# The second layer of the last two token chunks as seven block products, five of them in float32r

## The chip, the cores and the metric

The kernel runs on one core of a Trainium2 chip, as one launch. A core has TensorE (PE in the profile; its weight loads are listed apart, as PEld), VectorE (DVE), ScalarE (ACT), GpSimd (POOL) and SyncE (SP), each with its own queue of instructions, two on-chip memories (SBUF, and PSUM, which matmuls write) and DMA queues to the device's memory. The metric is the device time of one execution in microseconds.

## The reference

Attention over 8 batches of 8 heads, 576 positions of 64 values each, with a local mask for heads 0 to 3 and a strided one for heads 4 to 7, followed by a feed-forward layer on the 4608 tokens of 512 values:

```
scores = scale * np.matmul(q, k.transpose(0, 1, 3, 2))
...
attn = np.exp(scores)
attn = attn / (np.sum(attn, axis=-1, keepdims=True) + 1e-09)
...
h = x @ w_in            # 4608 x 512  times  512 x 2048
r = np.maximum(h, 0.0)
g = r * r
return (g @ w_out)      # 4608 x 2048  times  2048 x 512
```

The change concerns only the last line, `g @ w_out`, for the last 1024 tokens. Inputs and output are float32.

## The kernel before

The attention leaves its result `x`, transposed and in bf16, in four tiles `xt` (128 of the 512 values by 4608 tokens). The feed-forward layer takes the tokens in nine chunks of 512. For each chunk, `mm1` (lines 731 to 746) makes one group for each of 16 slices of 128 hidden values: four matmuls of 512 columns into one of two PSUM banks, `nc.scalar.activation(r, ph, AF.Relu)` on ACT into one of four `r` buffers, and, queued one group later by `later(1, ...)`, the square on DVE into `g[:, ff, :]`. `g` has two buffers, so that chunk c + 2 writes where chunk c was. Then `mm2` (lines 750 to 769) makes the second layer: for each of four blocks of 128 tokens, 16 matmuls of 512 columns, four in a group, with a slice of `g` as the stationary operand and `w_out_b[:, ff, :]` as the moving one; ACT copies the bank to a `y` buffer and SP's queue sends it to the output.

`last_y` (lines 775 to 790) does the last 128 tokens of the last chunk in pieces of 256, 128 and 128 columns, so that the first pieces leave while the last is computed.

The whole program is one list of groups (lines 947 to 972). With c from 2 on, groups 32c to 32c + 15 are chunk c's first layer, and the next 16 are its second layer. The attention of later batches is placed between the groups by a table written out by hand, `PLAN` (lines 23 to 165): at each group number, the steps to be issued ahead of it. Every engine runs its instructions in the order in which this list issues them. The last steps of the plan are at groups 188 (`G7`, the last local scores), 197 to 202 (`s7.0` to `s7.2`, the last strided scores), 198 to 206 (`D28` to `E29`) and 209 to 217 (`x7.0` to `x7.2`, the last strided values). From group 218 on there is only the feed-forward layer: the second layer of chunk 6 ends at group 223, chunk 7 is groups 224 to 255, and chunk 8 groups 256 to 287.

All tiles of the attention (staging, transposed q and k, `es`, `vl_all`, `vbds`, `kbds` and others) live in pools that stay open to the end of the kernel. PSUM has eight banks: `banks["ph"]` holds two, used by `mm1` and by most of `mm2`; `banks["pt"]` holds the others, used by the attention's steps and free at the end.

Lines that the prediction names: `L739` is the matmul of the first layer, `L761` and `L786` those of the second, `L745` the relu, `L746` the square, `L765` and `L789` the copies of results out of PSUM, `L583`, `L607` and `L621` matmuls of the steps `G`, `s` and `x`, `L705` a step of the local attention on DVE, `L426` the last load on POOL's queue, and `L884`, `L886` and `L898` the mask and the clearing of tiles on POOL early in the kernel.

Of the kernel before, what the change touches and what calls it, by code (L numbers as in the profile page):

```python
# [8 lines left out]
FP32 = mybir.dt.float32  # L9
BF16 = mybir.dt.bfloat16  # L10
AF = mybir.ActivationFunctionType
ALU = mybir.AluOpType
# [155 lines left out]
def kernel(  # L168
# [9 lines left out]
    nc = tc.nc  # L178
    B, H, S, D = q.shape
    d_model, d_ff = moe_w_in.shape  # L180
    T = B * S
# [4 lines left out]
    NL = S // QL  # L186
# [4 lines left out]
    VP = 72  # L191
    SR = 80
    NP2 = STRIDE // 2
    NG = 5
    NB = NP2 + NG + 1
    W3 = 3 * NA
    RW = STRIDE * D
    ER = S + 32

    singles = ctx.enter_context(tc.tile_pool(name="singles", bufs=1))  # L200
    qk_in = ctx.enter_context(tc.tile_pool(name="qk_in", bufs=4))
    qkT = ctx.enter_context(tc.tile_pool(name="qkT", bufs=4))
    v_st = ctx.enter_context(tc.tile_pool(name="v_st", bufs=1))
    rv_pool = ctx.enter_context(tc.tile_pool(name="rv_pool", bufs=3))
    small = ctx.enter_context(tc.tile_pool(name="small", bufs=4))
    xl_pool = ctx.enter_context(tc.tile_pool(name="xl_pool", bufs=4))
    g_pool = ctx.enter_context(tc.tile_pool(name="g_pool", bufs=2))
    r_pool = ctx.enter_context(tc.tile_pool(name="r_pool", bufs=4))
    y_pool = ctx.enter_context(tc.tile_pool(name="y_pool", bufs=4))

    PS = bass.MemoryType.PSUM
    strTs = {nm: ctx.enter_context(tc.tile_pool(name=f"strT{nm}", bufs=n)) for nm, n in (("q", 2), ("k", 1))}
# [25 lines left out]
    NV = 4  # L238
# [4 lines left out]
    vl_all = singles.tile([128, NV, 2, NL, VP], BF16, name="vl")  # L243
    vls = [vl_all[:, i] for i in range(NV)]

    vbds = [singles.tile([128, NB, 128], BF16, name=f"vb{i}") for i in range(2)]
    kbds = [singles.tile([128, NB, 128], BF16, name=f"kb{i}") for i in range(2)]
    ones_bd = singles.tile([128, 128], BF16)
    mask_bd = singles.tile([128, 1, W3], BF16)
    str_rows_t = {nm: singles.tile([SR, RW], BF16, name=f"{nm}_t") for nm in "qk"}  # L250
    kTl = [singles.tile([128, 32 + S], BF16, name=f"kTl{i}") for i in range(NV)]
    es01 = singles.tile([128, 4 * ER], BF16, name="e01")
    es = [es01[:, 0:2 * ER], es01[:, 2 * ER:]] + [singles.tile([128, 2 * ER], BF16, name=f"e{i}") for i in (2, 3)]
# [213 lines left out]
    def later(n, fn, key=None):  # L467
        pending.append((clock[0] + n, key, fn))

    def run_due(test):  # L470
        due = [x for x in pending if test(x)]
        for x in due:
            pending.remove(x)
        for x in sorted(due, key=lambda x: x[0]):
            x[2]()

    def tick():
        clock[0] += 1
        run_due(lambda x: x[0] <= clock[0])
# [229 lines left out]
    def step_E(u, copy=None):  # L709
# [14 lines left out]
        copy(xt[p][:, b * S:(b + 1) * S], px)  # L724
        st.pop(u)

    gs = {}

    phs = {}

    def mm1(c, ff, kks=range(4), order=range(4), pool=None):
        if ff == 0 and c not in gs:
            gs[c] = g_pool.tile([128, 16, 512], BF16, name="g_sb")
        g = gs[c]
        if kks[0] == order[0]:
            phs[ff] = bank(pool or "ph")
        ph = phs[ff]
        for kk in kks:
            nc.tensor.matmul(ph, w_in_b[:, kk, 128 * ff:128 * (ff + 1)],  # L739
                             xt[kk][:, 512 * c:512 * (c + 1)],  # L740
                             start=(kk == order[0]), stop=(kk == order[-1]))
        if kks[-1] != order[-1]:
            return
        r = r_pool.tile([128, 512], BF16, name="r")
        nc.scalar.activation(r, ph, AF.Relu)  # L745
        later(1, lambda: nc.vector.tensor_tensor(g[:, ff, :], r, r, op=ALU.mult))  # L746

    ys = {}

    def mm2(c, i, pool=None):  # L750
        j, part = divmod(i, 4)
        g = gs[c]
        if part == 0:
            if pool == "pt":
                ys[c, j] = bank("pt")
                banks["pt"].remove(ys[c, j])
            else:
                ys[c, j] = bank(pool or "py")
        py = ys[c, j]
        for ff in range(4 * part, 4 * part + 4):  # L760
            nc.tensor.matmul(py, g[:, ff, 128 * j:128 * (j + 1)], w_out_b[:, ff, :],  # L761
                             start=(ff == 0), stop=(ff == 15))
# [8 lines left out]
    NCH = T // 512  # L771
    A, V, G = nc.scalar.copy, nc.vector.tensor_copy, nc.gpsimd.tensor_copy
    ENG = {"a": A, "v": V, "g": G}

    def last_y(c, j, i):
        g, r0 = gs[c], 512 * c + 128 * j
        if i == 0:
            ys[c, j] = y_pool.tile([128, 512], FP32, name="y")
        y = ys[c, j]
        cols = (slice(0, 256), slice(0, 256), slice(256, 384), slice(384, 512))[i]  # L780
        ffs = (range(0, 8), range(8, 16), range(16), range(16))[i]
        if i != 1:
            ys[c, j, i] = bank("ph")
        py = ys[c, j, 0 if i == 1 else i]
        for ff in ffs:
            nc.tensor.matmul(py[:, cols], g[:, ff, 128 * j:128 * (j + 1)], w_out_b[:, ff, cols],  # L786
                             start=(ff == 0), stop=(ff == 15))
        if i:
            (V if i == 3 else A)(y[:, cols], py[:, cols])  # L789
            (nc.scalar if i == 2 else nc.sync).dma_start(out=out[r0:r0 + 128, cols], in_=y[:, cols])  # L790

    def warm(n):
        if n:
# [153 lines left out]
    groups = []  # L947

    def add(c, kind, i, pool=None):
        if kind == 0:  # L950
            groups.append(lambda: None)
        elif kind == 1:
            groups.append(lambda: mm1(c, i, pool=pool))
        elif c == NCH - 1 and i >= 12:
            groups.append(lambda: last_y(c, i // 4, i % 4))
        else:
            groups.append(lambda: mm2(c, i, pool))

    for ff in range(16):
        add(0, 1, ff, {NP: "pt", 8: "py"}.get(ff)) if ff >= NP else add(0, 0, ff)  # L960
    for part in range(4):
        for j, pool in ((0, "ph"), (1, "ph"), (2, None), (3, "pt")):
            add(0, 2, 4 * j + part, pool)
    for i in range(16):
        add(1, 1, i)
    for i in range(16):
        add(1, 2, i, "ph")
    for c in range(2, NCH):
        for i in range(16):
            add(c, 1, i)  # L970
        for i in range(16):
            add(c, 2, i, "ph")

    plan = {}
    for line in PLAN.strip().splitlines():
        n, words = line.split(":")
        plan.setdefault(int(n), []).extend(words.split())
    for n, g in enumerate(groups):
        if n == 32:
            banks["pt"] += banks.pop("py")  # L980
        for word in plan.get(n, ()):
            run_step(word)
        g()
        tick()
    for _ in range(4):
# [31 lines left out]
```

## Time and profile before

| | us |
|---|---|
| median of 3 runs | 299.06 (298.43 to 301.52) |
| the profiled execution | 299.14 |
| its span in the profile | 297.4 |
| TensorE busy | 287.8 |
| VectorE busy | 180.3 |
| ScalarE busy | 170.5 |
| GpSimd busy | 73.3 |

The span is the time from the first instruction in the trace to the last; the execution took 1.7 us more than that. A row of the page's fifth part names the line, the engine, the operation, what it writes and reads (partitions by elements, type), how often it runs, its busy time and the mean duration of one. A matmul's drawn duration is longer than its share of the stream, since matmuls are pipelined; the pace is read from start to start. In the 40 slices a digit is the busy share of a slice in tenths. A row of the timeline has a start, a length and an instruction, or several alike in one.

### The profile page before, as it was taken

Reading aid. Unit: us, or ns where it says so; the run is one execution under the profiler, and the core shown is the slowest. Engines: PE = TensorE matmul, PEld = TensorE weight load, DVE = VectorE, ACT = ScalarE, POOL = GpSimd, SP = SyncE. Lnnn points to the kernel's source line nnn. Section 1 sums busy time; section 2 is a strip of 40 time slices with the busy share of each in tenths; the row PEclk is TensorE's granted clock in tenths of the full one; section 3 lists DMA queues with packets and bytes.
Section 4 is the critical chain, followed back from the end, with each engine's and each line's share of the span. In section 5 each row is a group of like instructions: output and inputs, shape, how many; then the busy total and the mean of one; then the engine's idle time right before and its main releaser. Section 6 shows DMA issues by size and latency. Waiting matters only on the chain.

```text
span 297.4 us, 5621 instructions
## 1 busy us (share of the span) xinstructions
PE 287.8 (97%) x2112; PEld 144.6 (49%) x2148; DVE 180.3 (61%) x465; ACT 170.5 (57%) x318; POOL 73.3 (25%) x107
## 2 busy tenths in 40 slices
PE   7989999999999999999999999999999999999994
PEld 2644555544545454444454445544544444444444
DVE  5557689697777769779367936776575334004300
ACT  3758846774668636764577447744764266127411
POOL 8874743014513036065105700000000000000000
PEclk9999999999999999999999999999999999999999
DMA  7999999999999999999998999411011100020012
GB/s 146 183 207 204 189 199 189 156 224 204 168 179 179 123 164 199 160 144 188 179 128 125 177 149 145 82 55 73 35 31 47 71 37 0 35 89 20 0 71 73
DMA packets 91724, 37.38 MB, mean 126 GB/s; under 512 B 77549, under 2 KB 85831, under 8 KB 91697
## 3 DMA queue, kind: packets, MB, share of 16 engines
q0 software_dynamic: 50608, 18.33, 55.8%
q1 hardware_dynamic: 40944, 18.62, 32.3%
q8 instruction: 17, 0.28, 0.4%
q14 instruction: 11, 0.08, 0.1%
q10 hardware_dynamic: 144, 0.07, 0.1%
HBM read 37.22 MB, written 9.44 MB: 157 GB/s over the span
## 4 chain that ended last, share of the span: by engine, by line
PE 94%; DMA 2%; issue 1%; DVE 1%; ACT 0%; POOL 0%; DVEq 0%; POOLq 0%
PE psb L739 42%; PE psb L761 40%; DMA w_out_b<-in_k_dram 2%; PE psb L699 2%; PE psb L621 1%; PE psb L607 1%; PE psb L786 1%; PE psb L618 1%; PE psb L583 1%; PE psb L538 1%; PE psb L486 1%; DVE xt L668 0%; PE psb L508 0%; PE psb L333 0%; DVE x_l L688 0%
## 5 line engine op out<-in xcount | busy, mean ns | idle before, releaser
L739 PE MATMUL psb<-xt,w_in_b 128*128 128x512 bf16 x558 | 132.1, 379 | 1.2 <-DVE xt L668 0.2
L761 PE MATMUL psb<-w_out_b,g_sb 128*128 128x512 bf16 x542 | 125.3, 379 | 1.2 <-issue 0.5
L745 ACT ACTIVATE r<-psb 128x512 bf16<-128x512 f32 x144 | 85.3, 599 | 37.9 <-PE psb L739 32.8
L746 DVE TENSOR_TENSOR g_sb<-r 128x512 bf16<-128x512 bf16 x144 | 60.4, 423 | 68.5 <-ACT r L745 67.2
L739 PEld LDWEIGHTS <-w_in_b 128*128 128x128 bf16 x576 | 53.2, 97 | 58.9 <-issue 1.4
L761 PEld LDWEIGHTS <-g_sb 128*128 128x128 bf16 x560 | 52.0, 98 | 57.9 <-DVE g_sb L746 0.3
L765 ACT COPY y<-psb 128x512 f32<-128x512 f32 x35 | 20.6, 588 | 51.6 <-PE psb L761 48.6
L631 DVE TENSOR_TENSOR xt<-psb,rv 64x144 bf16<-64x144 f32 x84 | 34.0, 405 | 12.7 <-ACT rv L624 11.6
L623 ACT ACTIVATE rv<-psb 128x432 f32<-128x432 f32 (+1 forms) x21 | 10.5, 501 | 12.8 <-PE psb L618 12.8
L705 DVE TENSOR_TENSOR x_l<-psb,rinv 96x384 bf16<-96x384 f32 x28 | 15.5, 553 | 1.0
L361 POOL DMA_DIRECT2D q_t<-in_q_dram x6 | 3.3, 544 | 45.8 <-DMA qT_s<-q_t 44.9
L594 ACT ACTIVATE e<-psb 128x384 bf16<-128x384 f32 x30 | 12.0, 513 | 4.2 <-PE psb L583 4.2
L608 ACT ACTIVATE e<-psb 128x432 bf16<-128x432 f32 (+1 forms) x21 | 10.4, 496 | 4.0 <-PE psb L607 4.0
L637 DVE TENSOR_TENSOR xt<-psb,rv 64x270 bf16<-64x270 f32 (+1 forms) x28 | 11.0, 433 | 2.5 <-ACT rv L624 2.3
L290 POOL DMA_DIRECT2D q_l<-in_q_dram x16 | 12.0, 754 | 1.6 <-DMA q_l<-in_q_dram 1.4
L290 POOL DMA_DIRECT2D k_l<-in_k_dram x16 | 11.7, 736 | 1.6 <-DMA v_st<-in_v_dram 1.5
L624 ACT ACTIVATE rv<-rv 128x432 f32<-128x432 f32 (+1 forms) x21 | 11.2, 533 | 0.7
L590 DVE TENSOR_TENSOR e<-e,mask_all 128x576 bf16<-128x576 bf16 x20 | 8.4, 456 | 4.9 <-ACT e L594 4.9
L699 PEld LDWEIGHTS <-e 128*128 128x128 bf16 x168 | 8.0, 97 | 4.6
L361 POOL DMA_DIRECT2D k_t<-in_k_dram x6 | 3.2, 536 | 25.0 <-DMA kT_s<-k_t 22.9
L699 PE MATMUL psb<-vl,e 128*128 128x65 bf16 x168 | 9.0, 193 | 0.0
L607 PEld LDWEIGHTS <-kb 128*128 128x128 bf16 x154 | 6.8, 96 | 4.5
(119 smaller groups left out, 213.5 us busy)
## 6 DMA issues: line engine op xcount, KB each, us to landing
out_dram<-y SPq DMA_DIRECT2D x35, 256.0 KB, 4.2
w_out_b<-in_moe_w_out_dram POOLq DMA_DIRECT2D x4, 512.0 KB, 15.1
q_t<-in_q_dram POOLq DMA_DIRECT2D x7, 288.0 KB, 7.3
k_t<-in_k_dram POOLq DMA_DIRECT2D x7, 288.0 KB, 6.9
vl<-in_v_dram POOLq DMA_DIRECT2D x6, 288.0 KB, 7.7
v_st<-in_v_dram POOLq DMA_DIRECT2D x7, 216.0 KB, 6.8
w_in_b<-in_moe_w_in_dram POOLq DMA_DIRECT2D x2, 704.0 KB, 14.3
k_l<-in_k_dram POOLq DMA_DIRECT2D x16, 72.0 KB, 7.0
```

Of the source, the lines that this page charges most:

```text
L290: nc.gpsimd.dma_start(out=t[:, :, hh, :], in_=src[b, 2 * p + hh].rearrange("(t p) d -> p t d", p=QL))
L594: nc.scalar.activation(e[:, row, 4 * QL * i:4 * QL * (i + 1)], bk[row][i][:, 0:4 * QL], AF.Exp, scale=scale)
L624: nc.scalar.activation(rv, rv, AF.Exp, scale=-1.0)
L631: nc.vector.tensor_tensor(to[:, :, NJ * part:NJ * (part + 1), par], of, by, op=ALU.mult)
L637: nc.vector.tensor_tensor(t, of[:, g:, :, lo:lo + k], by[:, g:, :, lo:lo + k], op=ALU.mult)
L699: nc.tensor.matmul(po[:, n, :], e[:, c:c + 128], rhs[:, NL * part + n, 0:D + 1], start=True, stop=True)
L705: nc.vector.tensor_tensor(x, po[0:QL, :, 0:D], rinv[0:QL].to_broadcast([QL, NL, D]), op=ALU.mult)
L739: nc.tensor.matmul(ph, w_in_b[:, kk, 128 * ff:128 * (ff + 1)], xt[kk][:, 512 * c:512 * (c + 1)], start=(kk == order[0]), stop=(kk == order ...
L745: nc.scalar.activation(r, ph, AF.Relu)
L746: later(1, lambda: nc.vector.tensor_tensor(g[:, ff, :], r, r, op=ALU.mult))
L761: nc.tensor.matmul(py, g[:, ff, 128 * j:128 * (j + 1)], w_out_b[:, ff, :], start=(ff == 0), stop=(ff == 15))
L765: nc.scalar.copy(y, py)
```

## The change

For chunks 7 and 8 (`SEVEN`) the second layer is computed as a 2 by 2 by 2 block product with seven block multiplications. Tokens are split in pairs of 128 (t = 0, 1, within each half u of the chunk), hidden values in 0 to 1023 and 1024 to 2047, output columns in two times 256. With A11 and A12 the two hidden halves of the first 128 tokens, A21 and A22 those of the second 128, and B11 to B22 the blocks of `w_out`:

```
S1 = A21 + A22   S2 = S1 - A11   S3 = A11 - A21   S4 = A12 - S2
T1 = B12 - B11   T2 = B22 - T1   T3 = B22 - B12   T4 = B21 - T2
P1 = A11 B11  P2 = A12 B21  P6 = S2 T2  P7 = S3 T3  P4 = A22 T4  P5 = S1 T1  P3 = S4 B22
C11 = P1 + P2   C12 = P1 + P6 + P5 + P3   C21 = P1 + P6 + P7 + P4   C22 = P1 + P6 + P7 + P5
```

B21 is the lower left block, `w_out_b[:, 8:16, 0:256]`. The numbers are those of the code: products 1 and 2 have bf16 operands, `g` and `w_out_b`; the other five take operands that are sums, or a block copied to float32, held as float32r.

Five things are new:

- `weight_sums` (groups 204 to 223, one step at each) makes T1, a copy of B22, T3, T2 and T4 on POOL, in four pieces of 512 elements a partition each: 20 instructions. Before the first of them the pools of q and k (`rows`) are closed, and the new tiles take their memory; each waits for what used that memory.
- `squares` takes the place of the square in `mm1` for these chunks. For the slices 8 to 15 it makes, out of `r`, the square of the second tokens as float32r (`S["a"]`) and that of the first tokens as bf16, both on DVE, then S3 on DVE and S1, S2 and S4 on POOL, 256 elements each. Its tiles take the memory of the other attention pools (`att`).
- The first layer's order in these chunks is 0, 8, 1, 9, ..., 7, 15.
- `mm2_7` does one product of one half, eight matmuls of 256 columns, in the order 1, 2, 6, 7, 4, 5, 3, each for u = 0 and then u = 1. Products 2, 7 and 3 go on adding in the bank of the product before them on that bank. ACT copies the bank after 1 and 2; after the others DVE adds the bank and an earlier part of `y`.
- `last_y` is gone; in the last product, two additions of 128 columns and three DMAs (of 256, 128 and 128 columns) end the kernel.

```diff
     def mm1(c, ff, kks=range(4), order=range(4), pool=None):
...
         nc.scalar.activation(r, ph, AF.Relu)
+        if c in SEVEN:
+            later(1, lambda: squares(c, ff, r))
+            return
         later(1, lambda: nc.vector.tensor_tensor(g[:, ff, :], r, r, op=ALU.mult))
+
+    SEVEN = (NCH - 2, NCH - 1)
+    ts, ss = {}, {}
+
+    def weight_sums(step):
+        F32R = mybir.dt.float32r
+        if not ts:
+            rows.close()
+            late = ctx.enter_context(tc.tile_pool(name="late", bufs=1, side="right", reuse_waits="tile"))
+            for nm in ("1", "2", "3", "4", "b"):
+                ts[nm] = late.tile([128, 8, 256], F32R, name=f"t{nm}")
+        nm, i = "1b324"[step // 4], 2 * (step % 4)
...
+        if nm == "b":
+            nc.gpsimd.tensor_copy(t["b"], b22)
+            return
+        x, y = {"1": (b12, b11), "3": (b22, b12), "2": (b22, t["1"]), "4": (b21, t["2"])}[nm]
+        nc.gpsimd.tensor_tensor(t[nm], x, y, op=ALU.subtract)
+
+    def squares(c, ff, r):
+        g, i = gs[c], ff % 8
...
+        if ff < 8:
+            nc.vector.tensor_tensor(g[:, ff, :], r, r, op=ALU.mult)
+            return
+        S = {k: x[:, i] for k, x in ss.items()}
+        r = r.rearrange("p (u t c) -> p u t c", u=2, t=2)
+        a1, a2 = (g[:, k, :].rearrange("p (u t c) -> p u t c", u=2, t=2) for k in (i, ff))
+        nc.vector.tensor_tensor(S["a"], r[:, :, 1], r[:, :, 1], op=ALU.mult)
+        nc.vector.tensor_tensor(a2[:, :, 0], r[:, :, 0], r[:, :, 0], op=ALU.mult)
+        nc.vector.tensor_tensor(S["3"], a1[:, :, 0], a1[:, :, 1], op=ALU.subtract)
+        nc.gpsimd.tensor_tensor(S["1"], a1[:, :, 1], S["a"], op=ALU.add)
+        nc.gpsimd.tensor_tensor(S["2"], S["1"], a1[:, :, 0], op=ALU.subtract)
+        nc.gpsimd.tensor_tensor(S["4"], a2[:, :, 0], S["2"], op=ALU.subtract)
+
+    ORDER7 = "1 2 6 7 4 5 3".split()
+
+    def mm2_7(c, i):
+        n, u = ORDER7[i // 2], i % 2
...
+        for k in range(8):
+            a = g[:, k, t0] if n == "1" else g[:, 8 + k, t0] if n == "2" else \
+                ss[{"6": "2", "7": "3", "4": "a", "5": "1", "3": "4"}[n]][:, k, u]
+            b = w_out_b[:, k, lo] if n == "1" else w_out_b[:, 8 + k, lo] if n == "2" else \
+                ts[{"6": "2", "7": "3", "4": "4", "5": "1", "3": "b"}[n]][:, k]
+            nc.tensor.matmul(pa, a, b, start=k == 0 and n not in "273", stop=k == 7, skip_group_check=True)
+        if n in "12":
+            nc.scalar.copy((y2 if n == "1" else y1)[:, lo], pa)
+            return
...
+        if n == "3" and c == NCH - 1 and u:
+            nc.sync.dma_start(out=out[r0:r0 + 128, lo], in_=y1[:, lo])
+            for h, eng in ((0, nc.scalar), (128, nc.sync)):
+                nc.vector.tensor_tensor(to[:, h:h + 128], pa[:, h:h + 128], by[:, h:h + 128], op=ALU.add)
+                eng.dma_start(out=out[r0:r0 + 128, 256 + h:384 + h], in_=to[:, h:h + 128])
+            return
+        nc.vector.tensor_tensor(to, pa, by, op=ALU.add)
...
-        elif c == NCH - 1 and i >= 12:
-            groups.append(lambda: last_y(c, i // 4, i % 4))
+        elif c in SEVEN:
+            groups.append(lambda: mm2_7(c, i) if i < 14 else None)
...
-            add(c, 1, i)
+            add(c, 1, i // 2 + 8 * (i % 2) if c in SEVEN else i)
...
+        if 204 <= n < 224:
+            weight_sums(n - 204)
```

More of the change, by code (lines that the diff above doesn't have):

```diff
@@ L200 @@
     singles = ctx.enter_context(tc.tile_pool(name="singles", bufs=1))
[L201 to L204, printed above, removed]
     small = ctx.enter_context(tc.tile_pool(name="small", bufs=4))
-    xl_pool = ctx.enter_context(tc.tile_pool(name="xl_pool", bufs=4))
     g_pool = ctx.enter_context(tc.tile_pool(name="g_pool", bufs=2))
@@ L209 @@
     y_pool = ctx.enter_context(tc.tile_pool(name="y_pool", bufs=4))
+    att = ctx.enter_context(ExitStack())
+    rows = ctx.enter_context(ExitStack())
+    att_singles = att.enter_context(tc.tile_pool(name="att_singles", bufs=1))
+    rv_pool = att.enter_context(tc.tile_pool(name="rv_pool", bufs=3))
+    xl_pool = att.enter_context(tc.tile_pool(name="xl_pool", bufs=4))
+    row_singles = rows.enter_context(tc.tile_pool(name="row_singles", bufs=1, side="right"))
+    qk_in = rows.enter_context(tc.tile_pool(name="qk_in", bufs=4, side="right"))
+    qkT = rows.enter_context(tc.tile_pool(name="qkT", bufs=4, side="right"))
+    v_st = rows.enter_context(tc.tile_pool(name="v_st", bufs=1, side="right"))
     PS = bass.MemoryType.PSUM
-    strTs = {nm: ctx.enter_context(tc.tile_pool(name=f"strT{nm}", bufs=n)) for nm, n in (("q", 2), ("k", 1))}
+    strTs = {nm: rows.enter_context(tc.tile_pool(name=f"strT{nm}", bufs=n, side="right")) for nm, n in (("q", 2), ("k", 1))}
     psum = ctx.enter_context(tc.tile_pool(name="psum", bufs=1, space=PS))
@@ L242 @@
     mask_str = singles.tile([SP_, 1, SP_], BF16)
-    vl_all = singles.tile([128, NV, 2, NL, VP], BF16, name="vl")
+    vl_all = att_singles.tile([128, NV, 2, NL, VP], BF16, name="vl")
     vls = [vl_all[:, i] for i in range(NV)]
-    vbds = [singles.tile([128, NB, 128], BF16, name=f"vb{i}") for i in range(2)]
-    kbds = [singles.tile([128, NB, 128], BF16, name=f"kb{i}") for i in range(2)]
+    vbds = [att_singles.tile([128, NB, 128], BF16, name=f"vb{i}") for i in range(2)]
+    kbds = [row_singles.tile([128, NB, 128], BF16, name=f"kb{i}") for i in range(2)]
     ones_bd = singles.tile([128, 128], BF16)
     mask_bd = singles.tile([128, 1, W3], BF16)
[L250 to L253, printed above, removed]
+    str_rows_t = {nm: row_singles.tile([SR, RW], BF16, name=f"{nm}_t") for nm in "qk"}
+    kTl = [row_singles.tile([128, 32 + S], BF16, name=f"kTl{i}") for i in range(NV)]
+    es01 = att_singles.tile([128, 4 * ER], BF16, name="e01")
+    es = [es01[:, 0:2 * ER], es01[:, 2 * ER:]] + [att_singles.tile([128, 2 * ER], BF16, name=f"e{i}") for i in (2, 3)]
     xt = [singles.tile([128, T], BF16, name=f"xt{p}") for p in range(4)]
@@ L725, in step_E @@
         st.pop(u)
+    NCH = T // 512
     gs = {}
@@ L731, in mm1 @@
     def mm1(c, ff, kks=range(4), order=range(4), pool=None):
-        if ff == 0 and c not in gs:
+        if c not in gs:
             gs[c] = g_pool.tile([128, 16, 512], BF16, name="g_sb")
@@ L745, in mm1 @@
         nc.scalar.activation(r, ph, AF.Relu)
+        if c in SEVEN:
+            later(1, lambda: squares(c, ff, r))
+            return
         later(1, lambda: nc.vector.tensor_tensor(g[:, ff, :], r, r, op=ALU.mult))
+    SEVEN = (NCH - 2, NCH - 1)
[8 more added lines that the diff above has]
+        nm, i = "1b324"[step // 4], 2 * (step % 4)
+        lo, hi = slice(i, i + 2), slice(8 + i, 10 + i)
+        b11, b12 = w_out_b[:, lo, 0:256], w_out_b[:, lo, 256:512]
+        b21, b22 = w_out_b[:, hi, 0:256], w_out_b[:, hi, 256:512]
+        t = {k: x[:, lo] for k, x in ts.items()}
+        if nm == "b":
[3 more added lines that the diff above has]
+        nc.gpsimd.tensor_tensor(t[nm], x, y, op=ALU.subtract)
@@ new lines, in squares @@
+    def squares(c, ff, r):
+        g, i = gs[c], ff % 8
+        if not ss:
+            att.close()
+            late = ctx.enter_context(tc.tile_pool(name="sums", bufs=1, reuse_waits="tile"))
+            for nm in ("1", "2", "3", "4", "a"):
+                ss[nm] = late.tile([128, 8, 2, 128], mybir.dt.float32r, name=f"s{nm}")
+        if ff < 8:
[10 more added lines that the diff above has]
+        nc.gpsimd.tensor_tensor(S["4"], a2[:, :, 0], S["2"], op=ALU.subtract)
@@ new lines @@
+    ORDER7 = "1 2 6 7 4 5 3".split()
+    def mm2_7(c, i):
+        n, u = ORDER7[i // 2], i % 2
+        g, r0 = gs[c], 512 * c + 256 * u
+        t0 = slice(256 * u, 256 * u + 128)
+        if n == "1":
+            ys[c, u] = [y_pool.tile([128, 512], FP32, name="y") for _ in range(2)]
+            ys[c, u, "p"] = [bank("pt")]
+        if n == "6":
+            ys[c, u, "p"].append(bank("pt"))
+        y1, y2 = ys[c, u]
+        lo, hi = slice(0, 256), slice(256, 512)
+        pa = ys[c, u, "p"][n not in "124"][:, lo]
+        for k in range(8):
[7 more added lines that the diff above has]
+            return
+        to, by = {"6": (y1[:, hi], y2[:, lo]), "7": (y2[:, hi], y2[:, lo]), "4": (y2[:, lo], y2[:, hi]),
+                  "5": (y2[:, hi], y2[:, hi]), "3": (y1[:, hi], y1[:, hi])}[n]
+        if n == "3" and c == NCH - 1 and u:
[5 more added lines that the diff above has]
+        nc.vector.tensor_tensor(to, pa, by, op=ALU.add)
+        if n in "53":
+            r0 += 128 * (n == "5")
+            nc.sync.dma_start(out=out[r0:r0 + 128, :], in_=y2 if n == "5" else y1)
@@ L769, in mm2 @@
             nc.sync.dma_start(out=out[r0:r0 + 128, :], in_=y)
-    NCH = T // 512
     A, V, G = nc.scalar.copy, nc.vector.tensor_copy, nc.gpsimd.tensor_copy
     ENG = {"a": A, "v": V, "g": G}
[L775 to L790, printed above, removed]
     def warm(n):
```

## The prediction

> **What bounds the kernel now.** I read the page first: the busy times, the slices, the chain that ended last.
>
> ```profile
> span 297.4 us, 5621 instructions
> PE 287.8 (97%) x2112; PEld 144.6 (49%) x2148; DVE 180.3 (61%) x465; ACT 170.5 (57%) x318; POOL 73.3 (25%) x107
> POOL 8874743014513036065105700000000000000000
> PEclk9999999999999999999999999999999999999999
> PE 94%; DMA 2%; issue 1%; DVE 1%; ACT 0%; POOL 0%; DVEq 0%; POOLq 0%
> ```
>
> TensorE is busy 97% of the span at full clock and 94% of the chain; every other engine has room, and POOL does nothing in the last 40% of the span. So the time is the time of the matmul stream, and work taken off it counts in full as long as nobody makes it wait. Next the chain of waits from 236 us, for the stages that the change touches (start, length, what):
>
> ```profile
> 252.04 7.55 PE psb L761 x35
> ...
> 265.85 4.53 PE psb L739 x21
> ...
> 279.67 1.51 PE psb L761 x7
> ...
> 290.03 3.55 PE psb L786 x48
> ...
> 293.65 0.29 DVE y L789
> ```
>
> Second layer of chunk 7: 265.85 - 252.04 = 13.81 us. Of chunk 8: 290.03 + 3.55 - 279.67 = 13.91 us. Together 27.7 us without a gap, and this is all that the change can shorten. The timeline from 238 us shows the first layer of chunk 7:
>
> ```profile
> 237.63 0.38 PE L761 MATMUL psb<-w_out_b,g_sb 128*128 128x512 bf16 x1
> 238.06 4.48 PE L739 MATMUL psb<-xt,w_in_b 128*128 128x512 bf16 x20
> ...
> 239.76 0.43 DVE L746 TENSOR_TENSOR g_sb<-r 128x512 bf16<-128x512 bf16 x1 [5.14 <-ACT r L745]
> ```
>
> Twenty matmuls in 4.48 us, of which the last is drawn 0.38 long, as one of 512 columns is: (4.48 - 0.38) / 19 = 0.216 us from start to start. A group of four takes 0.863 us, and in that time DVE has one multiply of 0.43.
>
> **What TensorE gains.** A chunk's second layer becomes 2 halves x 7 products x 8 matmuls of 256 columns, 112, so 224 for both, 64 in bf16 and 160 in float32r. The trace has the 256-column bf16 form in the last block:
>
> ```profile
> L786 PE MATMUL psb<-w_out_b,g_sb 128*128 128x128 bf16 x32 | 1.9, 219 | 0.0
> L786 PE MATMUL psb<-w_out_b,g_sb 128*128 128x256 bf16 x16 | 1.9, 273 | 0.0
> ```
>
> The stretch of 3.55 us holds 32 x 128 + 16 x 256 = 8192 columns, 0.43 ns each, so 0.111 us for 256, weight load included (48 loads, one for each matmul, all beside them). 224 x 0.111 = 24.9 us against 27.7: a gain of 2.85 us, if float32r goes at the bf16 pace. No row of the trace is float32r. Below, 0.111: one column in the same step. Above, 0.216: the row with the same number of bytes, 512 columns of bf16. Built, each float32r product is one weight load and one matmul, not several passes, so I take 0.111, the row with the same column count. 0.216 would cost 160 x 0.105 = 16.8 us; it is a rival.
>
> **What the new operands cost.** In the first layer of chunks 7 and 8 the groups now go 0, 8, 1, 9, ...; that is free, all weights being there. But a pair of groups (1.73 us of TensorE) now asks DVE for four operations: the multiply of 512, a multiply of 256 to float32r, one of 256 to bf16, a subtraction of 256 to float32r; and POOL for three of 256 with two inputs each.
>
> ```profile
> L746 DVE TENSOR_TENSOR g_sb<-r 128x512 bf16<-128x512 bf16 x144 | 60.4, 423 | 68.5 <-ACT r L745 67.2
> L705 DVE TENSOR_TENSOR x_l<-psb,rinv 96x384 bf16<-96x384 f32 x28 | 15.5, 553 | 1.0
> 238.00:252.00 14.00, 13.90 (x65) 6.34 (x65) 6.11 (x15) 9.54 (x16) 0.00 (x0) 1.00 0.05 20
> ```
>
> (The third row is a stage by engine: PE, PEld, DVE, ACT, POOL busy, with counts.) With a 32-bit operand DVE takes 0.29 us for 128 (the `L789` row) and 0.553 for 384, so 0.42 for 256; for 256 in bf16, between 0.29 (128 in 32 bits) and 0.423, I take 0.29. Back to back, DVE's operations overlap by some 0.08 us: 3 x 0.34 + 0.21 = 1.23 us a pair. DVE alone would hold 1.73.
>
> POOL's two-input operation is in no row. The nearest:
>
> ```profile
> L898 POOL MEMSET kb<- 128x1408 f32 x2 | 2.6, 1291 | 0.0
> L1001 POOL MEMSET const-float32-0.0<- 128x1 f32 x1 | 0.1, 98 | 0.3 <-issue 0.3
> ```
>
> 0.10 us fixed and (1.291 - 0.098) / 1407 = 0.85 ns an element for one pass. If both reads hide in that pass, 256 cost 0.31 us; if two reads and a write follow one another, 0.75. I take the middle, 0.53, and keep both ends. [...]
>
> Now the row that speaks against this change. It is early in the kernel, where POOL and DVE work at once (start, length):
>
> ```profile
> 28.14 0.23 POOL L884 TENSOR_SCALAR_AFFINE_SELECT mask_bd<-mask_bd 64x54 bf16<-64x54 bf16 x1
> 28.44 0.51 POOL L886 TENSOR_SCALAR_AFFINE_SELECT mask_bd<-mask_bd 64x54 bf16<-64x54 bf16 x1
> ...
> 29.34 0.47 POOL L886 TENSOR_SCALAR_AFFINE_SELECT mask_bd<-mask_bd 64x54 bf16<-64x54 bf16 x1
> ```
>
> ```profile
> 28.42 0.43 DVE L746 TENSOR_TENSOR g_sb<-r 128x512 bf16<-128x512 bf16 x1
> ...
> 29.29 0.42 DVE L746 TENSOR_TENSOR g_sb<-r 128x512 bf16<-128x512 bf16 x1
> ```
>
> The same 64x54 select takes 0.23 us alone and 0.51 or 0.47 when it starts just after a DVE multiply with two SBUF operands; it ends 0.10 us after that multiply. So POOL waited for DVE. [...]
>
> I take it that both wait. All of the new operations read SBUF on both engines. A pair then needs 1.23 + 3 x (0.53 - 0.10) = 2.52 us of turns in 1.73 us: 0.79 too long, 8 x 0.79 = 6.3 us a chunk. TensorE feels it because DVE's multiply frees the four `r` buffers and product 1 needs all of `g`'s first half; about 1.0 us lies beside the first two products, which want nothing from POOL. That leaves 5.3 us a chunk, 10.7 for two. With 0.31 a pair needs 1.86 us and nothing is left (0); with 0.75 it needs 3.18, 8 x 1.45 - 1 = 10.6 a chunk, 21 for two.
>
> The twenty weight sums stand alone in POOL's queue, whose last entry before was long ago. They wait for the memory that they take over:
>
> ```profile
> 169.59 0.62 POOL L426 DMA_DIRECT2D v_st<-in_v_dram  x1
> ```
>
> ```profile
> 204.04 0.62 PE psb L583 x24
> ...
> 217.81 0.15 PE psb L607 x6
> ...
> 232.03 0.16 PE psb L621 x6
> ```
>
> Eight of 512 may go once the local scores at 204 us are through, twelve after the last strided scores at 218 us: at 0.10 + 2 x 0.43 = 0.96 us each, done by 230 us, before the first activation sums at 240 us and long before product 6 at 256 us. They take turns with DVE too, but DVE is busy for 61% of the span and can give way, so I cost it at nothing; bound 0 to 1 us. The buffers of the activation sums were last used by the values' matmuls at 232 us: no wait either. POOL's queue holds nothing behind these waits but the sums themselves.
>
> Between products the banks are read by ACT and DVE:
>
> ```profile
> 291.81 0.37 ACT L789 COPY y<-psb 128x256 f32<-128x256 f32 x1 [1.16 <-PE psb L786]
> ```
>
> ACT's copies (0.37 us for 256) and DVE's additions (0.42) each lie behind the other half's product of 0.89 us, so a bank is free again when it is wanted; without that cover each of 28 would cost about 0.5 us.
>
> The end: two DVE additions of 128 follow one another instead of one copy, and 0.5 MB more of output leaves in the last 2 us.
>
> ```profile
> out_dram<-y SPq DMA_DIRECT2D x3, 256.0 KB, 2.0
> ```
>
> 256 KB landed within 2.0 us at the median, so most of it is out of the way: +0.3 us, between 0.2 and 1.
>
> The sum: the profiled execution took 299.14 us for its span of 297.4, and the median of the runs is 299.06, so I start at 299.1: 299.1 - 2.85 + 10.7 + 0.3 = **307 us**. Within this mechanism, from 297 (POOL at 0.31) to 318 (at 0.75).
>
> **The rivals.**
> First, no wait at all: the two engines overlap, or POOL's operation is near its lower end. For it: POOL alone has 24 x 0.53 = 12.7 us of work in the 18 us until product 6 reads its last sum. Then 299.1 - 2.85 + 0.3 = 296.6. Against it: the select rows.
> [...]
> Third, the change does not save TensorE time: float32r goes at 0.216. 296.6 + 16.8 = 313.4, and up to 324 if the turns cost as forecast too. Against it: one pass each. For it: no row shows a 4-byte operand. [...]
>
> **How the numbers follow.** Turns between DVE and POOL: 0.45. No wait: 0.30. POOL late alone: 0.08. Float32r slow: 0.15. Something else, such as a wait in the new end that I don't see: 0.02. The range 296.2 to 318 takes in the no-wait case with its 0.4 us of tail, and the forecast up to POOL's dear end; outside are most of the slow-float32r cases and a little on each side. The likeliest case's own range is 299 to 318. One per cent, about what a measurement here can tell from no change, is 3.0 us: faster is under 296.1, which even the no-wait case reaches only if the tail costs nothing and 256 columns go below 0.111: 0.06. Within: most of the no-wait case, most of the second rival, and the cheap end of the forecast: 0.35. Slower: 0.59.
>
> **What would show it.** In the profile after: float32r matmuls of `mm2_7` start 0.11 us apart (or 0.21: third rival). In 240 to 255 us POOL's three operations at 0.4 to 0.7 us, longer where a DVE operation is under way, DVE's multiplies ended late, and gaps on TensorE in the first layer of chunks 7 and 8 released by ACT, in turn released by DVE: forecast right. [...] The forecast is wrong if DVE's rows keep their length while POOL runs.

## The result, and the profile after

| | before | after |
|---|---|---|
| median | 299.14 us (298.43 to 301.52, 4 runs) | 315.76 us (314.36 to 320.19, 4 runs) |
| profiled execution | 299.14 | 315.79 |
| its span | 297.4 | 314.1 |

The ratio after to before is 1.0525, with a 95% interval from 1.0446 to 1.0605: slower, by about 16.6 us where the forecast said 7.9. The run of 320.19 us went at a lower granted clock (0.967, the others 0.983 to 0.988), and runs of this kind are left out of all ratios. The page of the changed kernel begins like this (the third line is POOL's in the 40 slices):

```profile
span 314.1 us, 5958 instructions
PE 295.2 (94%) x2212; PEld 157.6 (50%) x2212; DVE 225.9 (72%) x517; ACT 168.6 (54%) x317; POOL 130.6 (42%) x175
...
POOL 8965542017130180660055000083970885048810
PEclk9999999999999999999999999999999995999899
...
PE 78%; DVE 16%; ACT 2%; issue 2%; DMA 1%; SPq 0%; DVEq 0%; ACTq 0%
```

TensorE's share of the chain that ended last has gone from 94% to 78%, and DVE, which had 1%, has 16%. POOL is busy where it did nothing before. And the clock, full throughout before, falls in two places of the last fifth.

The chain of waits says where the time went. First chunk 6 (start, length, what), after:

```profile
208.69 4.32 PE psb L744 x20
...
218.95 1.06 DVE g_sb L754
...
221.20 2.59 DVE g_sb L754 x2
...
240.50 1.74 PE psb L744 x8
```

and the start of the same stage before:

```profile
208.22 4.32 PE psb L739 x20
```

Before, the stage took 238.06 - 208.22 = 29.8 us with TensorE alone on the chain; after, 240.50 - 208.69 = 31.8, and DVE's squares, 0.42 us each before, stand on the chain with 1.1 to 1.3. POOL's last twelve sums of weights run beside and after them, from 218.57 to 233.4 us. Then chunks 7 and 8:

```profile
254.93 0.81 DVE g_sb L785
...
257.59 0.81 DVE g_sb L785
...
261.10 14.63 PE psb L816 x105
275.73 1.76 PE psb L744 x8
...
296.48 14.04 PE psb L816 x105
```

The first layer is now a chain of DVE: from one square of the first half to the next, a pair of groups, 257.59 - 254.93 = 2.66 us, where TensorE needs 1.73. Product 1's eighth matmul waits for the last of these squares, and from there the 105 matmuls that are left run without a stop. TensorE's own timeline shows the stops, and what follows them (in brackets the idle time before, and who ended it):

```profile
255.72 0.82 PE L816 MATMUL psb<-w_out_b,g_sb 128*128 128x256 bf16 x6
258.45 0.28 PE L816 MATMUL psb<-w_out_b,g_sb 128*128 128x256 bf16 x1 [1.91 <-DVE g_sb L785]
261.10 5.17 PE L816 MATMUL psb<-w_out_b,g_sb 128*128 128x256 bf16 x25 [2.37 <-DVE g_sb L785]
266.03 4.03 PE L816 MATMUL psb<-t,s 128*128 128x256 f32 x32
```

The 25 bf16 matmuls after the second stop take 266.03 - 261.10 = 4.93 us, 0.197 each rather than 0.111. The windows of this stretch, and one of chunk 8, tell why (columns: length, then PE, PEld, DVE, ACT and POOL busy with counts, then the granted clock, DMA share and GB/s):

```profile
256.54:258.95 2.41, 0.29 (x2) 0.10 (x1) 2.41 (x5) 0.60 (x1) 2.13 (x3) 1.00 0.00 0
258.96:265.78 6.82, 4.68 (x23) 3.31 (x24) 3.93 (x7) 1.12 (x3) 4.20 (x6) 0.50 0.00 0
265.79:268.00 2.21, 2.21 (x20) 2.19 (x19) 0.42 (x1) 0.37 (x1) 0.00 (x0) 1.00 0.00 0
...
296.51:299.91 3.40, 3.40 (x17) 2.40 (x18) 1.75 (x3) 0.74 (x2) 2.51 (x4) 0.50 0.00 0
```

From 256.54 to 261.10 us there is one matmul; in the middle of that stretch the granted clock falls to 0.50, and it stays there for 6.8 us. In chunk 8 it is at 0.50 for 3.4 us. The 80 float32r matmuls that follow, from 266.03 to the next stage at 275.73, come 9.70 / 80 = 0.121 us apart.

With these rows the whole difference can be laid out, stage against stage (chunk 8 read in the same way; its 25 slow matmuls took 4.32 us):

| part | working | forecast | measured |
|---|---|---|---|
| up to chunk 6's first layer | 208.69 - 208.22 | 0 | +0.5 |
| weight sums beside chunk 6 | 31.8 - 29.8 | 0 | +2.0 |
| turns, chunk 7 | 261.10 - 240.50, less 13.98 + 7 x 0.111 | +5.3 | +5.8 |
| turns, chunk 8 | 296.48 - 275.73, less 13.82 + 7 x 0.111 | +5.3 | +6.2 |
| matmuls at half clock | 4.93 + 4.32, less 50 x 0.111 | 0 | +3.7 |
| second layers at 0.111 each | 224 x 0.111 - 27.7 | -2.85 | -2.85 |
| float32r above 0.111 | 2 x (9.7 - 80 x 0.111) | 0 | +1.7 |
| the end | 314.1 - 310.52, less 297.4 - 293.58 | +0.3 | -0.25 |
| sum | | +8 | +16.8 |

The spans differ by 314.1 - 297.4 = 16.7 us. The first row is no effect of the change: two kernels below reach that place at 207.7 us.

DVE's rows by shape, for the last two chunks of the changed kernel:

```profile
L785 DVE TENSOR_TENSOR g_sb<-r 128x512 bf16<-128x512 bf16 x16 | 13.3, 830 | 6.2 <-ACT r L750 6.2
L790 DVE TENSOR_TENSOR sa<-r 128x256 fp32r<-128x256 bf16 x16 | 13.2, 825 | 1.0 <-ACT r L750 1.0
```

L785 is the very multiply that took 0.423 before. And POOL beside DVE, in two pieces of the timeline, POOL's first:

```profile
252.07 0.73 POOL L794 TENSOR_TENSOR s<-s,g_sb 128x256 fp32r<-128x256 f32 x1
252.88 0.73 POOL L795 TENSOR_TENSOR s<-g_sb,s 128x256 fp32r<-128x256 bf16 x1
```

```profile
252.20 0.89 DVE L785 TENSOR_TENSOR g_sb<-r 128x512 bf16<-128x512 bf16 x1
253.01 0.89 DVE L790 TENSOR_TENSOR sa<-r 128x256 fp32r<-128x256 bf16 x1
253.82 0.28 DVE L791 TENSOR_TENSOR g_sb<-r 128x256 bf16<-128x256 bf16 x1
```

Read the ends. L794 ends at 252.80, and DVE's L785, begun at 252.20, ends 0.29 us after it. L795, begun at 252.88, ends at 253.61, which is 0.52 after L785's end; DVE's L790 ends 0.29 after that. So they alternate, some 0.29 us for DVE and 0.52 for POOL, and each of these drawn lengths holds a wait for the other engine. L791, which begins in POOL's pause after L795, takes its plain 0.28.

### The profile page after: what moved, and what is told of

Same layout as the page of the kernel before. It is cut to its first block, busy times and chain, and to the rows that moved or that the text cites. A ratio compares the mean times of both kernels' runs of the same rounds, so it can differ in the third digit from the quotient of the medians.

```text
span 314.1 us, 5958 instructions
## 1 busy us (share of the span) xinstructions
PE 295.2 (94%) x2212; PEld 157.6 (50%) x2212; DVE 225.9 (72%) x517; ACT 168.6 (54%) x317; POOL 130.6 (42%) x175
## 4 chain that ended last, share of the span: by engine, by line
PE 78%; DVE 16%; ACT 2%; issue 2%; DMA 1%; SPq 0%; DVEq 0%; ACTq 0%
PE psb L846 30%; PE psb L744 29%; PE psb L816 9%; DVE g_sb L785 4%; DVE s L792 3%; DVE g_sb L754 2%; DVE sa L790 2%; DMA g_sb<-in_k_dram 1%; PE psb L703 1%; ACT r L750 1%; DVE g_sb L791 1%; PE psb L625 1%; PE psb L542 1%; PE psb L611 1%; PE psb L622 1%
## 5 line engine op out<-in xcount | busy, mean ns | idle before, releaser
L744 PE MATMUL psb<-xt,w_in_b 128*128 128x512 bf16 x576 | 134.9, 379 | 2.0 <-ACT r L750 1.7
L846 PE MATMUL psb<-w_out_b,g_sb 128*128 128x512 bf16 x448 | 103.5, 379 | 1.5 <-DVE g_sb L754 1.5
L744 PEld LDWEIGHTS <-w_in_b 128*128 128x128 bf16 x576 | 53.1, 97 | 62.0 <-issue 6.6
L754 DVE TENSOR_TENSOR g_sb<-r 128x512 bf16<-128x512 bf16 x112 | 53.6, 487 | 30.2 <-ACT r L750 29.1
L635 DVE TENSOR_TENSOR xt<-psb,rv 64x144 bf16<-64x144 f32 x84 | 34.1, 406 | 10.7 <-ACT rv L628 9.6
L850 ACT COPY y<-psb 128x512 f32<-128x512 f32 x28 | 16.5, 591 | 33.3 <-PE psb L846 33.1
L775 POOL TENSOR_TENSOR t<-w_out_b 128x512 fp32r<-128x512 bf16 x8 | 10.1, 1288 | 39.9 <-PE psb L587 34.8
L793 POOL TENSOR_TENSOR s<-g_sb,sa 128x256 fp32r<-128x256 bf16 x16 | 11.3, 709 | 29.1 <-DVE sa L790 19.0
L828 DVE TENSOR_TENSOR y<-psb,y 128x256 f32<-128x256 f32 x19 | 8.1, 425 | 17.0 <-PE psb L816 8.8
L816 PE MATMUL psb<-w_out_b,g_sb 128*128 128x256 bf16 x64 | 11.9, 360 | 8.6 <-DVE g_sb L785 8.6
L785 DVE TENSOR_TENSOR g_sb<-r 128x512 bf16<-128x512 bf16 x16 | 13.3, 830 | 6.2 <-ACT r L750 6.2
L594 DVE TENSOR_TENSOR e<-e,mask_all 128x576 bf16<-128x576 bf16 x20 | 11.5, 617 | 4.7 <-ACT e L598 4.7
L790 DVE TENSOR_TENSOR sa<-r 128x256 fp32r<-128x256 bf16 x16 | 13.2, 825 | 1.0 <-ACT r L750 1.0
L792 DVE TENSOR_TENSOR s<-g_sb 128x256 fp32r<-128x256 bf16 x16 | 13.5, 843 | 0.0
```

The costliest lines, as they stand in the source:

```text
L635: nc.vector.tensor_tensor(to[:, :, NJ * part:NJ * (part + 1), par], of, by, op=ALU.mult)
L790: nc.vector.tensor_tensor(S["a"], r[:, :, 1], r[:, :, 1], op=ALU.mult)
L792: nc.vector.tensor_tensor(S["3"], a1[:, :, 0], a1[:, :, 1], op=ALU.subtract)
L816: nc.tensor.matmul(pa, a, b, start=k == 0 and n not in "273", stop=k == 7, skip_group_check=True)
```

## The experiments

Three theories stood after this. Turns: DVE's operations with two SBUF operands and POOL's wait for one another. Format: DVE is slow because it writes float32r. Capacity: the added work is too much for the stage wherever it is put. For the rest of the loss there were the half clock and the weight sums.

**Without POOL's sums.** POOL makes only the first of the eight slices of each activation sum.

```
         nc.vector.tensor_tensor(S["3"], a1[:, :, 0], a1[:, :, 1], op=ALU.subtract)
+        if i:
+            return
         nc.gpsimd.tensor_tensor(S["1"], a1[:, :, 1], S["a"], op=ALU.add)
...
-                ss[...][:, k, u]
+                ss[...][:, 0 if n in "653" else k, u]
```

> POOL forms the sums S1, S2 and S4 only for the first pair of each chunk, and products 6, 5 and 3 read that one slice eight times; the other 42 POOL operations are left out. Turns on a common port (theory): DVE's four operations fall from 0.83, 0.83, 0.34 and 0.84 us to 0.42, 0.42, 0.29 and 0.42, the pairs come every 1.73 us instead of 2.66, TensorE doesn't stop, the clock stays full in the first two products, and both chunks lose 7 us each: 301 us. Rival, DVE's long operations are their own price (float32r writes on DVE take 0.83 us whatever POOL does): DVE stays at 2.66 us a pair and the time at 315 us. What then is left above 299 is the weight sums (about 2 us) and the pace of float32r matmuls.

299.02 us (298.87 to 300.13), ratio 1.0014 to the kernel before (0.9998 to 1.003). DVE's row and the chain of this kernel:

```profile
L785 DVE TENSOR_TENSOR g_sb<-r 128x512 bf16<-128x512 bf16 x16 | 7.6, 477 | 6.2 <-ACT r L750 6.2
```

```profile
239.76 13.97 PE psb L744 x64
253.73 12.96 PE psb L818 x112
266.68 14.05 PE psb L744 x64
280.73 12.97 PE psb L818 x112
```

The 0.48 is a mean: the second of these squares in each chunk runs beside the first pair's sums, at 0.90, and the other fourteen take 0.41 to 0.43. The four DVE operations are all still there, float32r results too, and the first layers are back at 14.0 us, with the granted clock at 1.00 through both chunks: the stops and what followed them are gone with POOL's sums. What is left shows the products alone: 12.96 + 12.97 = 25.9 us against 27.7, a gain of 1.8, not 2.85. It is spent on the weight sums, which are all still made: chunk 6 takes 239.76 - 207.95 = 31.8 us here too. The time is 2 us under what was expected, mostly since the stops and the slow matmuls after them are 15.7 us in the table where the expectation had 14.

**POOL writes only.** In place of its three sums, POOL clears the same tiles with six memsets of 256 for each pair.

```
+        if i:
+            for nm in "112244":
+                nc.gpsimd.memset(S[nm].bitcast(FP32), 0.0)
+            return
         nc.gpsimd.tensor_tensor(S["1"], a1[:, :, 1], S["a"], op=ALU.add)
```

> As in the run without POOL's sums, but POOL writes the same slices with six memsets of 256 a pair, about 0.31 us each, so that it is as busy as with three sums (1.9 us a pair) and reads nothing. If only POOL's reads share DVE's second operand, DVE's operations stay at 0.42 and the time is that of the run without POOL's sums, about 301 us. If any POOL work holds DVE up, the pairs go back to about 2.6 us and the time to about 315 us.

299.48 us (298.82 to 305.64), ratio 1.0031 (0.9998 to 1.0065). Its rows for the two engines:

```profile
L795 POOL MEMSET s<- 128x256 f32 x84 | 23.8, 311 | 2.4
```

```profile
L785 DVE TENSOR_TENSOR g_sb<-r 128x512 bf16<-128x512 bf16 x16 | 7.6, 477 | 6.2 <-ACT r L750 6.2
```

POOL's 84 memsets keep it busy for 23.8 us beside DVE, and DVE's row is the same to the nanosecond as with these sums left out. So these memsets don't hold DVE up; the sums do, and a sum reads SBUF where a memset only writes it: L785 takes 0.83 us beside sums, 0.48 beside memsets. What the two engines share no run shows. Who of the two has to wait is another question; the last run below has a row on it.

**The sums on DVE.** The three sums move from POOL to DVE; nothing else changes.

```
-        nc.gpsimd.tensor_tensor(S["1"], a1[:, :, 1], S["a"], op=ALU.add)
-        nc.gpsimd.tensor_tensor(S["2"], S["1"], a1[:, :, 0], op=ALU.subtract)
-        nc.gpsimd.tensor_tensor(S["4"], a2[:, :, 0], S["2"], op=ALU.subtract)
+        nc.vector.tensor_tensor(S["1"], a1[:, :, 1], S["a"], op=ALU.add)
+        nc.vector.tensor_tensor(S["2"], S["1"], a1[:, :, 0], op=ALU.subtract)
+        nc.vector.tensor_tensor(S["4"], a2[:, :, 0], S["2"], op=ALU.subtract)
```

> Nothing left out: S1, S2 and S4 are made on DVE in place of POOL. Theory: no turns, but DVE alone needs 1.23 + 3 x 0.34 = 2.25 us a pair against 1.73: 0.52 x 8 - 1 = 3.2 us late in each chunk, so 301 + 6.4 = 307 us, with a shorter stop of TensorE. Rival, DVE's float32r operations cost 0.83 each by themselves: 4.5 us a pair and over 335 us.

313.7 us (313.03 to 314.33), ratio 1.0488 (1.0457 to 1.0518): slower than expected. DVE's rows, and TensorE's timeline:

```profile
L785 DVE TENSOR_TENSOR g_sb<-r 128x512 bf16<-128x512 bf16 x16 | 6.7, 419 | 6.2 <-ACT r L750 6.2
L790 DVE TENSOR_TENSOR sa<-r 128x256 fp32r<-128x256 bf16 x16 | 6.7, 419 | 0.9 <-ACT r L750 0.9
```

```profile
239.88 10.62 PE L744 MATMUL psb<-xt,w_in_b 128*128 128x512 bf16 x48
...
259.82 5.52 PE L816 MATMUL psb<-w_out_b,g_sb 128*128 128x256 bf16 x25 [2.18 <-DVE g_sb L785]
264.99 1.22 PE L816 MATMUL psb<-t,s 128*128 128x256 f32 x7
```

Every DVE operation is back at 0.42, the float32r ones too, so the theory of the format falls. But seven operations a pair are too much for 1.73 us: the chunk's first layer and seven matmuls took 259.82 - 239.88 = 19.9 us against 14.8, a loss of 5.2 where the turns cost 5.8. So capacity decides, and the turns are one way to run out of it: POOL's idle time was not there to be had. The pair itself, in the chain of waits:

```profile
247.12 0.34 DVE g_sb L785
...
248.69 0.43 DVE s L794
249.15 0.42 DVE s L795
249.58 0.34 DVE g_sb L785
```

A pair comes every 2.46 us. My expectation took 2.25, with the overlapped 0.34 for each operation of 256 to float32r and for the one of 512. An operation that needs nothing of the last does follow 0.34 after it. But L794 and L795 each read what the operation before them wrote, and L795 starts 0.46 after L794. The half clock follows here too, without any POOL sum beside it: 25 matmuls in 264.99 - 259.82 = 5.17 us, 0.207 each, and +3.6 us for both chunks, which was not expected. In chunk 8 the matmuls were back at 294.68 us and ran at full clock for 1.3 us before it fell:

```profile
294.68:295.98 1.30, 1.30 (x12) 1.18 (x13) 1.27 (x5) 0.48 (x2) 0.00 (x0) 1.00 0.00 0
295.99:299.39 3.40, 3.40 (x18) 2.59 (x17) 0.73 (x2) 1.00 (x3) 0.00 (x0) 0.50 0.02 5
```

**A quarter of the weight sums.** Five of the twenty are made, and the products read those again and again.

```
-        if 204 <= n < 224:
+        if 204 <= n < 224 and n % 4 == 0:
...
-                ts[{"6": "2", "7": "3", "4": "4", "5": "1", "3": "b"}[n]][:, k]
+                ts[{"6": "2", "7": "3", "4": "4", "5": "1", "3": "b"}[n]][:, k % 2]
```

> POOL makes only 5 of the 20 weight sums (the first piece of each), and the products read these two slices in turn; the other 15 are left out. Theory: they hold DVE's multiplies of chunk 6 up, which cost 2.0 us between 208 and 240 us; without them this stage goes back from 31.8 to about 30 us and the time from 315.8 to 314. Rival: the 2 us come from the changed placement of tiles or the new first-layer order, and stay.

313.2 us (312.24 to 313.53), ratio 1.0466 (1.0437 to 1.0495). The whole time hardly separates it from the changed kernel, whose interval overlaps; the stage does:

```profile
207.70 4.32 PE psb L744 x20
...
237.71 1.74 PE psb L744 x8
```

30.0 us for chunk 6, against 31.8 with all sums and 29.8 before them. The placement of the tiles and the new order of the first layer, the rival, are as in the changed kernel. So the weight sums cost the 2.0 us, by the same turns: they were priced at nothing because DVE had room in that stage.

**Float32r without turns.** ACT makes the square that goes to float32r, DVE two of POOL's sums in the first layer and the third one during the products, and a one-element copy on POOL holds the last twelve weight sums back until chunk 6's squares are made.

```
+        if step == 8:
+            gate = small.tile([128, 1], BF16, name="gate")
+            nc.gpsimd.tensor_copy(gate, gs[NCH - 3][:, 15, 0:1])
...
-        nc.vector.tensor_tensor(S["a"], r[:, :, 1], r[:, :, 1], op=ALU.mult)
+        nc.scalar.activation(S["a"], r[:, :, 1], AF.Square)
...
+    def fourth(c, i):
...
-            groups.append(lambda: mm2_7(c, i) if i < 14 else None)
+            groups.append(lambda: (mm2_7(c, i) if i < 14 else None, fourth(c, i - 1) if 1 <= i < 9 else None))
```

> All seven products in float32r as changed, but no POOL operation beside DVE's: ACT squares the second tokens of the upper slices, DVE makes S3, S1 and S2 (0.34 + 0.21 + 3 x 0.34 = 1.57 us a pair, under 1.73), S4 follows on DVE during the products, and the twelve later weight sums wait on POOL until chunk 6's last square is done (some 224 us), 12 x 1.24 = 15 us until 239. Theory: no stop in the first layers, full clock, products at 0.111 in bf16 and 0.118 in float32r: 64 x 0.111 + 160 x 0.118 = 26.0 us for 27.7, and 296.5 to 297.5 us, or 0.3 to 0.8% under before. Rival: the chain from ACT to DVE is too long, or the weight sums, now later, hold up chunk 7, and it is 300 us or more.

298.19 us (297.72 to 307.06, 12 runs), ratio 0.9996 (0.997 to 1.0023): no difference that can be told, where about 2 us of gain was expected. The chain:

```profile
237.53 10.89 PE psb L744 x49
...
251.66 13.25 PE psb L822 x112
...
278.90 13.26 PE psb L822 x112
```

No stop is left, and the products take 13.25 us for each chunk: 1.2 us less than before for both together, of the 2.85 that bf16's pace would give. A gain of that size is little more than the interval of the whole time can show. All 80 matmuls in float32r are at about (13.25 - 32 x 0.111) / 80 = 0.121. With the waits gone, the float32r pace eats more than half of what the seventh product saves.

**All sums in bf16, and on DVE.** In bf16, A22 needs no copy of its own (product 4 reads `g`), nor does B22 (product 3 reads `w_out_b`), so a pair of groups is two multiplies of 512 and four sums of 256 on DVE. The sixteen weight sums are put on DVE too, at groups 208 to 223; POOL gets nothing.

```
-                ss[nm] = late.tile([128, 8, 2, 128], mybir.dt.float32r, name=f"s{nm}")
+                ss[nm] = late.tile([128, 8, 2, 128], BF16, name=f"s{nm}")
...
-        nc.vector.tensor_tensor(S["a"], r[:, :, 1], r[:, :, 1], op=ALU.mult)
-        nc.vector.tensor_tensor(a2[:, :, 0], r[:, :, 0], r[:, :, 0], op=ALU.mult)
...
-        nc.gpsimd.tensor_tensor(S["1"], a1[:, :, 1], S["a"], op=ALU.add)
+        nc.vector.tensor_tensor(S["1"], a1[:, :, 1], a2[:, :, 1], op=ALU.add)
...
-        if 204 <= n < 224:
-            weight_sums(n - 204)
+        if 208 <= n < 224:
+            weight_sums(n - 208)
```

> The same seven products with all sums in bf16 and all on DVE: 2 x 0.34 + 4 x 0.21 = 1.52 us a pair and some 0.1 for sums that wait on the one before, under 1.73; the sixteen weight sums on DVE in chunk 6's second layer, 0.34 us each; POOL does nothing. Theory: no stop, every product at 0.111: 24.9 us for 27.7, and 295.5 to 296.3 us, about 1% under before, 1 us under the float32r version. Rival: DVE's dependent sums take 0.45 each as in the run with sums on DVE, a pair comes to over 1.9 us, and it is 298 us or more. The rounding of sums to bf16 makes the output less exact.

295.96 us (295.6 to 296.92), ratio 0.9907 (0.9884 to 0.993). This one is faster than both kernels: by 0.7 to 1.2% than the one before. TensorE's timeline in the products:

```profile
255.50 3.66 PE L812 MATMUL psb<-t,s 128*128 128x256 bf16 x32
259.00 1.91 PE L812 MATMUL psb<-t,g_sb 128*128 128x256 bf16 x16
```

32 in 3.50 us, 0.109 each. The gain, 0.93% or 2.8 us, is about the 2.85 that the forecast had for TensorE. It isn't quite free of waits: products 1 and 2, from 251.78 us on, took 3.72 us, 0.2 over this pace, since product 1's eighth matmul still waits for a square. The price is that the sums, and so their rounding, are in bf16.

**Only the type.** The changed kernel with the sums in bf16 and everything else, POOL's part too, as it was.

```
-        F32R = mybir.dt.float32r
+        F32R = BF16
...
-                ss[nm] = late.tile([128, 8, 2, 128], mybir.dt.float32r, name=f"s{nm}")
+                ss[nm] = late.tile([128, 8, 2, 128], BF16, name=f"s{nm}")
```

> As changed, POOL's sums kept where they are, but all sums and their products in bf16 instead of float32r. Theory: turns depend on who reads what, not on the type: a POOL sum of 256 still takes about 0.67 us and a pair 3 x 0.67 plus the part of DVE's work that can't lie beside it, 2.3 to 2.6 us, so the stops and the half clock stay, and only the pace of the products (0.109 for 0.120, 1.8 us) and some of DVE's time come back: 309 to 314 us. Rival: the float32r writes are what makes the operations long; then a pair is under 1.8 us and it is 297 to 299 us.

306.14 us (303.96 to 307.74), ratio 1.0209 (1.0125 to 1.0293), less than expected. DVE's row for the last two chunks:

```profile
L785 DVE TENSOR_TENSOR g_sb<-r 128x512 bf16<-128x512 bf16 x16 | 13.3, 828 | 6.4 <-ACT r L750 6.4
```

0.83 again, in bf16 as in float32r (0.828 and 0.830): the turns didn't depend on the type here, and it is where the sums are made that loses the time. The pair takes 2.36 us by the timeline, as expected, since DVE's 256-column operations are shorter in bf16. What wasn't foreseen is that the weight sums cost nothing: chunk 6 takes 237.69 - 207.69 = 30.0 us. They began at 217.57 us here, released by a matmul of the strided scores, and at 205.31 in the changed kernel. So only four sums and the copies met DVE's squares of chunk 6; the other twelve sums began at 226.36, when those squares were done. The four held DVE up as before, two squares for 2.67 us. The copies did not. POOL's second copy, and DVE's squares beside it:

```profile
223.21 2.08 POOL L772 COPY tb<-w_out_b 128x512 bf16<-128x512 bf16 x1
```

```profile
223.40 1.42 DVE L754 TENSOR_TENSOR g_sb<-r 128x512 bf16<-128x512 bf16 x4
```

The squares take 1.42 / 4 = 0.36 us each. The copy takes 2.08, where the two after it, beside DVE operations that read PSUM, take 0.62 each, and it ends 0.47 us after the last square. So these engines do wait for one another here, but POOL does all of the waiting. The casts to float32r in the changed kernel, 0.80 us each from 210.39 us on, alternated with the squares, which took 0.83. Why a copy lets four squares pass where a sum or a cast gets its turn after each stays open; no run took them apart.

## Why the prediction was right, and where its size was wrong

**What bounds the kernel** was read rightly: work taken off TensorE counted in full, for in the bf16 kernel without POOL 2.8 us of the 2.85 came out.

**The mechanism** was the one forecast as likeliest. The select rows showed POOL behind DVE; the added step, that DVE waits for POOL as well, stood in no row of the kernel before, and the sum of the forecast took it as given. It is shown by the 0.83 us of L785 beside sums, and by its 0.42 to 0.48 when the sums go to DVE, are left out, or are replaced by memsets. A common port, of which the first expectation speaks, no run shows; what the trace of the changed kernel shows in its place is that the two engines' operations end by turns, 0.29 us for DVE and 0.52 for POOL.

**The turns** came to 12.0 us, forecast 10.7. The pair takes 2.66 us, not 2.52. The sum gave POOL's operation a turn of 0.53 - 0.10 = 0.43 us and DVE's three longer ones 0.34 each; the trace has 0.52 and 0.29, and 3 x (0.52 + 0.29) + 0.20 = 2.63. So two errors in part cancel. POOL's whole operation took 0.67 alone (the last L795 of chunk 7, at 263.49 us with DVE idle), so the middle of 0.31 and 0.75 was low.

**The stops' price is the step that failed.** The sum took the stops at their own length. The profile's page before showed a full clock in all slices, and I carried that over to a kernel in which TensorE waits. After the two stops the 25 next matmuls ran at 0.197 and 0.173 us, +3.7 us for both chunks. The kernel with the sums on DVE has such stops too, and a like pace after them, 0.207 and 0.158; the one without POOL's sums and the one with memsets have no stops in these chunks, and their clock stays at 1.00.

What brings the clock down, and what sets the 6.8 and 3.4 us at half, no run took apart. The two stops of a chunk are 1.91 and 2.37 us, with one matmul between them; in chunk 7 the clock fell at 258.96 us, before the matmuls were back at 261.10. In chunk 8 of the kernel with the sums on DVE, after stops of 1.70 and 2.18 us, it fell at 296.0 us, 1.3 us after the matmuls were back.

**The weight sums** were costed at 0, bounded by 1, and took 2.0. The sums took 1.15 to 1.37 us each, not 0.96. The reason given for the 0, that DVE has room, was true of DVE's average of 61% and false of that stage: DVE's squares there release TensorE directly, so squares that each end 0.6 us late or more add up to a stop, whatever room DVE has afterwards.

**Float32r's pace** was taken as 0.111, with 0.216 as a rival. It is 0.119 to 0.121: near the row with the same columns, but with so small a gain the 0.009 us matter, 1.7 of 2.85. The rival, 0.216, falls.

**The end** was forecast at +0.3 and gave -0.25: the two additions and the added output cost nothing that can be seen.

**The other rivals.** No wait at all would be 296.6, and needs L785 at 0.42. POOL late alone, with neither engine waiting for the other, would put the stop before product 6; the stops stand before product 1's last two matmuls, and product 6 starts without one at 266.03. Of the signs that were named, one was off: the large gaps were released by DVE, and ACT's were the small ones.

**The range** held in part by luck. Its upper part, to 318, stood for a dearer POOL operation. What filled it were three terms that the sum had at nothing: the half clock (3.7 us), the weight sums (2.0) and float32r's pace (1.7), beside turns of nearly the size forecast.

## What to carry to other kernels

An idle POOL was no free engine for sums beside a DVE that works on two SBUF operands: L785 took 0.83 us in place of 0.42, and a pair took 2.66 us on the two engines, 2.46 with all of it on DVE. So add both engines' times for the stage, as if one engine did them, and compare with the period in which the critical engine asks. In the four kernels with stops of TensorE, each of 1.1 to 2.4 us before product 1's last two matmuls, they cost more than their length: the 25 matmuls after them took 0.158 to 0.207 us each, 1.4 to 1.9 times the 0.111, and in the changed kernel the clock was at half for 6.8 us in chunk 7 and 3.4 in chunk 8. So look at the clock after a stop. Where a change saves one eighth of a short stage, a few per cent of pace decide it (0.009 us above 0.111 took 1.7 us of 2.85 here), so the pace of the new type is worth a measurement before anything else.

## What was not expected of the hardware

Float32r weight loads were drawn longer than bf16's here, 189 ns against 97 for L744's:

```profile
L816 PEld LDWEIGHTS psb<-t,s 128*128 128x128 f32 x96 | 11.6, 189 | 0.0
```

Whether the load is what sets the pace of 0.12 us wasn't tried. POOL's memsets, 84 of them, cost DVE nothing (L785 at 477 ns with them and without), where three sums for each pair nearly doubled the row (423 to 830 ns). And a bf16 copy on POOL let four of DVE's squares pass before it ended: 2.08 us, where the next two copies took 0.62 each.
